# Strided convolution with norm and GELU, forward and backward: outer sums added at eviction, and a first weight-gradient combination split by batches

## The chip, the cores and the metric

The kernel runs on one core of a Trainium2 chip. The metric is the device time of one execution in microseconds (us); the time before is the median of three runs. Engines are named as in the profile: PE is TensorE's matmul, PEld its weight load, DVE is VectorE, ACT is ScalarE, POOL is GpSimd, SP is SyncE, which here issues nearly all loads.

## What is computed

```python
def _fwd_reference(x, w, gn_gamma, gn_beta):      # x (2, 16000, 256), w (31, 256, 256), bf16
    L = (T - K) // s + 1                          # K = 31, s = 2: L = 7985
    h = jnp.einsum('blc,cd->bld', x[:, 0:s * L:s, :], w[0])
    for i in range(1, K):
        h = h + jnp.einsum('blc,cd->bld', x[:, i:i + s * L:s, :], w[i])
    mu = jnp.einsum('bld->bd', h)[:, None, :] / L
    var = jnp.einsum('bld->bd', (h - mu) ** 2)[:, None, :] / L
    h = (h - mu) / jnp.sqrt(var + 1e-5)
    h = h * gn_gamma[None, None, :] + gn_beta[None, None, :]
    return _gelu(h)

_out, _vjp = jax.vjp(_f, x, w, gn_gamma, gn_beta)
_grads = _vjp(grad_out)                           # outputs: out, dx, dw, dgamma, dbeta
```

A convolution of 31 taps with stride 2 over 256 channels, a normalisation over time for each channel, and a GELU; then the gradients of x (`out_1`), w (`out_2`), gamma and beta.

## The kernel before, in words

Three large products make up the matmul work: the convolution, the input gradient and the weight gradient. Each is cut by fast-convolution splits into three branches, two halves and their sum, which the code calls A, C_ and B_ (the sum). The splits nest, so a product has branches `br` and inside each leaves `lf`. They save matmuls and cost additions: of inputs (bf16, on DVE) and of partial results (fp32, in PSUM).

The stages run in this order: F0 (convolution of batch 0), F1 (convolution of batch 1, while batch 0 is normalised and goes through GELU and its derivative), G0 (input gradient of batch 0, chunks 0 to 2, while batch 1 is normalised), G1 (chunk 3 of batch 0 and all of batch 1), and W (weight gradient, nine combinations n = 0 to 8 of two levels of branches).

**What sets the order.** One planner, `Plan`, gets every operation in program order with a guessed cost, gives each a due time, and shifts it by a table `lead` (a number for each stage, kind of operation and function that adds it) and a second table `fine` (the same by part, a chunk or a combination). Each engine's list is then sorted by the shifted times, and each engine runs its list in order. All loads and most stores go through SP's queue, which is such a list too; a load also waits until its buffer is free. PSUM is a ring of four slots of two banks (`ring`, `slots4`).

**Input gradient** (`input_grad`, from `g_leaf` to `g_evac`). For each batch b, chunk c, half chunk pr and branch br, two slots px and pt are taken. First the leaf B_ goes into px: `g_three_b` runs four matmuls into one bank, ACT copies them to the other bank (L1353), and `g_three_ac` adds eight matmuls on top. Then `g_seed` prepares px and pt as starting values of the leaves C_ and A, which add their matmuls onto them, and `g_evac` takes each of these out. For br = B_ the result is kept in GRB, an fp32 buffer in SBUF. It is the outer sum that the branches A and C_ need, and there each seed adds it: L1393 in `plus`, one addition of 128x2048 that writes px + GRB to pt and px both. `keep` is ACT's copy (L833); the evictions of A and C_ write bf16 into HO, from which the output is stored. In batch 1, and in chunk 3 of batch 0, another form is used (`outer`, `both`, sets GO and GOC), in which matmuls make part of the outer sum; the change leaves that form as it is. Where the page says that PE L1326 waits for ACT L1353, the matmul of `g_three_ac` waits for the copy.

**Weight gradient** (`weight_grad`). For each n, four tiles xt of x (two batches, two halves) and, for each batch, tiles D2 and DO of the output's gradient (`d_tile`, loaded from the DRAM buffers `dl_d`) are needed. `w_add` (L1527) forms XSUM of the two halves, 128x4096 for each batch, `pair_x` (L1625 for both batches in one, L1629 for one batch) adds neighbouring rows, `leaf_d` (L1712) and `pair_d` (L1638) form differences of the gradient, and `w_pairs` runs 2 x 16 matmuls from the pairs; `w_single` and `w_leaf` add the rest. ACT spreads the result of `w_pairs` over a slot (L1654), `w_both` (L1662) adds a middle result, and `w_emit` (L1588) adds the last two terms, writes bf16 to one of the buffers WO and stores it. `place` turns through sets of buffers for the pairs (PD). All buffers lie at hand-given addresses in one tile `arena`, so a load for n = 0 can start when the last reader of what lay at that address before is done:

```python
    XSUM_ = [[sb(o, 8, 512) for o in v] for v in ((24576, 32768), (0, 8192))]
    D2E_ = [[sb(o + 5120 * i, 10, D) for i in range(2)] for o in (0, 127424)]
    D2O_ = [[sb(o + 10240 + 4608 * i, 9, D) for i in range(2)] for o in (0, 127424)]
```

(the first set is for n = 0, the second for n = 1 to 8).

## Time and profile before

| | us |
|---|---|
| runs | 1178.08, 1179.34, 1175.58 (median 1178.08) |
| profiled execution, device time | 1176.72 |
| span of that execution | 1174.9 |
| around the span (difference) | 1.8 |
| PE busy | 1133.9 |
| DVE busy | 980.1 |
| ACT busy | 568.8 |
| mean granted clock | 0.99 |

The profiled execution lies among the three runs. Its span is what the views divide up; the 1.8 us around it are outside every view. A window's row gives for a stretch of the span the busy time of each engine with its number of instructions, then the clock that TensorE was granted (1.00 is full speed), the mean busy share of the DMA engines, and GB/s. A group's row gives line, engine, operation, written and read tiles, shapes and count, then total busy time, mean ns of one, and the idle time of that engine just before such instructions with what ended it. In a timeline the idle time ahead of a piece stands in brackets.

### The profile page before, as it was taken

Reading aid. Unit: us, or ns where it says so; the run is one execution under the profiler, and the core shown is the slowest. Engines: PE = TensorE matmul, PEld = TensorE weight load, DVE = VectorE, ACT = ScalarE, POOL = GpSimd, SP = SyncE. Lnnn points to the kernel's source line nnn. Section 1 sums busy time; section 2 is a strip of 40 time slices with the busy share of each in tenths; the row PEclk is TensorE's granted clock in tenths of the full one; section 3 lists DMA queues with packets and bytes.
Section 4 is the critical chain, followed back from the end, with each engine's and each line's share of the span. In section 5 each row is a group of like instructions: output and inputs, shape, how many; then the busy total and the mean of one; then the engine's idle time right before and its main releaser. Section 6 shows DMA issues by size and latency. Waiting matters only on the chain.

```text
span 1174.9 us, 18909 instructions
## 1 busy us (share of the span) xinstructions
PE 1133.9 (97%) x7700; PEld 755.0 (64%) x7700; DVE 980.1 (83%) x861; ACT 568.8 (48%) x849; POOL 128.3 (11%) x221
## 2 busy tenths in 40 slices
PE   5999999999999999999999999999799999899997
PEld 4888899777777954444444444444388666566784
DVE  8998787699999998898886776876699897688996
ACT  1253454778776587897854666534222212211200
POOL 0000000000000002332242223223000000000000
PEclk8999999999999999999999999999999999999999
DMA  9475747979795799999988679576987836998574
GB/s 215 69 200 101 186 135 143 213 161 212 166 230 139 266 304 264 251 255 268 233 209 219 157 181 231 133 205 162 307 234 195 289 113 203 311 328 304 167 204 126
DMA packets 345806, 243.56 MB, mean 207 GB/s; under 512 B 233377, under 2 KB 316967, under 8 KB 341543
## 3 DMA queue, kind: packets, MB, share of 16 engines
q1 hardware_dynamic: 338615, 223.47, 71.5%
q0 software_dynamic: 7104, 18.89, 5.7%
q8 instruction: 60, 0.98, 0.3%
q14 instruction: 27, 0.22, 0.1%
HBM read 106.24 MB, written 80.25 MB: 159 GB/s over the span
## 4 chain that ended last, share of the span: by engine, by line
PE 84%; DVE 7%; ACT 4%; DMA 3%; issue 2%; SPq 0%; DVEq 0%; ACTq 0%
PE ps L738 32%; PE ps L1326 27%; PE ps L1559 25%; DMA arena<-in_x_dram 2%; DVE ps L1393 2%; ACT arena L833 1%; DVE arena L696 1%; DVE arena L1393 1%; DVE arena L680 1%; ACT ps L1353 0%; ACT arena L1098 0%; DVE arena L1625 0%; DVE arena L1103 0%; DMA out_dram<-arena 0%; ACT arena L1124 0%
## 5 line engine op out<-in xcount | busy, mean ns | idle before, releaser
L1326 PE MATMUL ps<-arena 128*128 128x512 bf16 (+1 forms) x1920 | 415.6, 377 | 12.2 <-ACT ps L1353 5.0
L738 PE MATMUL ps<-arena 128*128 128x256 bf16 (+4 forms) x3460 | 406.9, 281 | 12.5 <-DVE arena L680 5.6
L738 PEld LDWEIGHTS <-arena 128*128 128x128 bf16 x3460 | 338.5, 99 | 80.8 <-DVE arena L680 6.5
L1326 PEld LDWEIGHTS <-arena 128*128 128x128 bf16 x1920 | 188.3, 98 | 238.3 <-issue 22.0
L1559 PE MATMUL ps<-arena 128*128 128x256 bf16 (+1 forms) x2320 | 312.2, 298 | 10.2 <-DVE arena L1625 8.3
L1559 PEld LDWEIGHTS <-arena 128*128 128x128 bf16 x2320 | 228.2, 99 | 94.4 <-DVE arena L1625 9.6
L833 ACT ACTIVATE arena<-ps 128x1024 f32<-128x1024 f32 (+1 forms) x143 | 145.5, 1021 | 294.6 <-PE ps L1326 108.4
L696 DVE TENSOR_TENSOR arena<-arena 128x2064 bf16<-128x2064 bf16 (+7 forms) x126 | 155.9, 1264 | 27.9 <-PE ps L738 27.4
L544 POOL DMA_DIRECT2D dld<-arena x144 | 104.7, 729 | 266.9 <-DMA arena<-arena 248.6
L1393 DVE TENSOR_TENSOR ps<-ps,arena 128x2048 f32<-128x2048 f32 x40 | 91.8, 2295 | 26.8 <-PE ps L1326 20.2
L1113 DVE TENSOR_TENSOR arena<-arena 128x2048 bf16<-128x2048 bf16 (+1 forms) x80 | 95.6, 1195 | 13.0 <-ACT arena L1107 6.4
L1527 DVE TENSOR_TENSOR arena<-arena 128x4096 bf16<-128x4096 bf16 x38 | 86.0, 2284 | 23.4 <-DMA arena<-in_x_dram 20.3
L1279 DVE TENSOR_TENSOR arena<-arena 128x1032 bf16<-128x1032 bf16 (+1 forms) x120 | 84.2, 725 | 21.9 <-PE ps L1326 16.1
L853 ACT ACTIVATE arena<-ps 128x512 bf16<-128x512 f32 (+1 forms) x64 | 37.0, 580 | 45.1 <-PE ps L738 44.4
L1654 ACT COPY ps<-ps 128x256 f32<-128x256 f32 x54 | 19.3, 357 | 79.0 <-PE ps L1559 77.3
L553 POOL MEMSET arena<- 128x128 bf16 (+11 forms) x40 | 8.4, 243 | 424.8 <-DVE arena L696 140.1
L1393 DVE TENSOR_TENSOR arena<-ps,arena 128x2048 f32<-128x2048 f32 x16 | 36.6, 2287 | 19.5 <-ACT arena L833 15.9
L808 ACT ACTIVATE arena<-ps 128x512 f32<-128x512 f32 x56 | 29.7, 601 | 38.2 <-DVE ps L818 16.3
L1638 DVE TENSOR_TENSOR arena<-arena 128x2048 bf16<-128x2048 bf16 x38 | 45.0, 1217 | 0.9 <-PE ps L1559 0.7
L1712 DVE TENSOR_TENSOR arena<-arena 128x4608 bf16<-128x4608 bf16 x18 | 45.5, 2549 | 0.0
L1103 DVE SCALAR_TENSOR_TENSOR arena<-arena 128x2048 bf16<-128x2048 bf16 (+1 forms) x16 | 35.8, 2236 | 10.9 <-ACT arena L1100 10.9
L774 ACT ACTIVATE ps<-ps 128x256 f32<-128x256 f32 x75 | 27.9, 372 | 29.4 <-PE ps L738 28.3
(80 smaller groups left out, 706.9 us busy)
## 6 DMA issues: line engine op xcount, KB each, us to landing
arena<-in_x_dram SPq DMA_DIRECT2D x40, 1024.0 KB
dld<-arena POOLq DMA_DIRECT2D x144, 128.0 KB, 3.9
arena<-hd SPq DMA_DIRECT2D x32, 512.0 KB
out_dram<-arena SPq DMA_DIRECT2D x14, 1024.0 KB
arena<-dld SPq DMA_DIRECT2D x18, 640.0 KB
arena<-dld SPq DMA_DIRECT2D x18, 576.0 KB
vl<-arena SPq DMA_DIRECT2D x36, 256.0 KB
arena<-vl SPq DMA_DIRECT2D x9, 1024.0 KB
```

The source lines that it names most:

```text
L544: lambda: e.dma_start(out=out, in_=in_), dma=np_ * ns / 16e3 * 1.03, ns=ns, tp=SH[pk], slack=slack)
L696: lambda: nc.vector.tensor_tensor(out=o, in0=a, in1=b, op=ALU.add))
L738: yield nc.tensor.matmul(ps[:, dh, cs], lhsT=wt, rhs=mv, start=s0, stop=False, skip_group_check=True)
L833: lambda: nc.scalar.activation(out=out, in_=ps, func=ACT.Copy, scale=scale))
L1113: add("DVE", dve(nf), [o], [a, b_], lambda: V.tensor_tensor(out=o, in0=a, in1=b_, op=op))
L1279: lambda: nc.vector.tensor_tensor(out=o, in0=a, in1=b, op=ALU.subtract))
L1326: yield nc.tensor.matmul(ps[:, e, 0:wide], lhsT=lt, rhs=mv, start=s0, stop=False, skip_group_check=True)
L1393: lambda: nc.vector.tensor_tensor(out=o, in0=a, in1=b, op=ALU.add))
L1527: add("DVE", dve(4096), [o], [a, b], lambda: nc.vector.tensor_tensor(out=o, in0=a, in1=b, op=ALU.add))
L1559: yield nc.tensor.matmul(ps[:, s, c0:c1], lhsT=lt, rhs=mv, start=s0, stop=False, skip_group_check=True)
L1638: add("DVE", dve(2048), [o], [u, v], lambda o=o, u=u, v=v: nc.vector.tensor_tensor(out=o, in0=u, in1=v, op=ALU.subtract))
L1712: add("DVE", dve(4608), [o], [u, v], lambda: nc.vector.tensor_tensor(out=o, in0=u, in1=v, op=ALU.subtract))
```

## The change

Three things change beside the two tables.

First, the input gradient's first batch (where neither `outer` nor `both` holds). The seed of the branches A and C_ becomes what it was for B_, a copy on ACT from px to pt, and the outer sum GRB is added at the eviction, on DVE, as PSUM is read.

```diff
-        elif br == B_:
+        else:
             keep(flat2(pt), flat2(px))
-        else:
-            o, i = both_ways()
-            plus(o, i, GRB.rearrange("p k e f -> p k (e f)"), [pt[:], px[:]], [px[:], GRB])
...
         k = (0 if br == A else 1) + (0 if lf == A else 2)
-        keep(ho[:, :, k, :], ps[:])
+        if (b, c, br) in GO or (b, c, pr) in GOC:
+            keep(ho[:, :, k, :], ps[:])
+        else:
+            g = GRB[:, 0 if lf == A else 1]
+            add("DVE", dve(1024, 1), [ho[:, :, k, :]], [ps[:], g],
+                lambda: nc.vector.tensor_tensor(out=ho[:, :, k, :], in0=ps[:], in1=g, op=ALU.add))
```

Second, the first combination of the weight gradient (n = 0) is split by batches, and its buffers lie elsewhere; for n = 1 to 8 the two halves of XSUM are no longer neighbours, so that `pair_x` runs as two instructions of 2048 there.

```diff
-    XS_ = [sb(o, 8, 512) for o in (165376, 86016, 190336, 40960)]
-    XT_ = [sb(o, 8, 512) for o in (24576, 173696, 32768, 182016)]
+    XS_ = [sb(o, 8, 512) for o in (165376, 86016, 182016, 0)]
+    XT_ = [sb(o, 8, 512) for o in (24576, 173696, 32768, 190336)]
-    XSUM_ = [[sb(o, 8, 512) for o in v] for v in ((24576, 32768), (0, 8192))]
-    D2E_ = [[sb(o + 5120 * i, 10, D) for i in range(2)] for o in (0, 127424)]
-    D2O_ = [[sb(o + 10240 + 4608 * i, 9, D) for i in range(2)] for o in (0, 127424)]
+    XSUM_ = [[sb(o, 8, 512) for o in v] for v in ((8192, 32768), (8192, 40960))]
+    D2E_ = [[sb(o, 10, D) for o in v] for v in ((24576, 40960), (127424, 132544))]
+    D2O_ = [[sb(o, 9, D) for o in v] for v in ((16384, 57344), (137664, 142272))]
...
-          for k, o, u in (("all", 16384, 73728), ("early", 110720, 118912), ("late", 57344, 65536))}
+          for k, o, u in (("all", 16384, 73728), ("early", 110720, 118912), ("late", 57344, 65536), ("first", 73728, 65536))}
...
+            if n == 0:
+                return PD[("first", "early", "late")[turn_[0] - 1]]
...
                 w_add(XSUM[b], xt[b, 0], xt[b, 1])
-            pair_x(pm, XSUM)
+                if n == 0:
+                    pair_x((pm[b],), (XSUM[b],))
+            if n:
+                pair_x(pm, XSUM)
...
+                if n == 0:
+                    for b in range(NB):
+                        o, u, v = DL[i3, b], D2[b][:, o_:o_ + 9], DO[b]
+                        add("DVE", dve(2304), [o], [u, v], lambda o=o, u=u, v=v: nc.vector.tensor_tensor(
+                            out=o, in0=u, in1=v, op=ALU.subtract))
+                    return
...
-            for h in range(2):
-                w_pairs(X[h], h, pm, DO, 1, 2)
+            if n == 0:
+                for b in range(NB):
+                    for h in range(2):
+                        w_pairs(X[h], h, pm, DO, 1, 2, True, ((b,),))
+            else:
+                for h in range(2):
+                    w_pairs(X[h], h, pm, DO, 1, 2)
...
-                        t = sb(8192 * r3 * seeded + 4096 * h, 1024, dt=FP32)
+                        t = sb((8192, 40960)[r3 * seeded] + 4096 * h, 1024, dt=FP32)
```

`w_pairs` takes the batches as groups and runs the matmuls of one group for both halves of the slot; ACT's copies follow the last group. `pair_d` runs four instructions of 1024 where the two batches' tiles lie apart (n = 0), in place of two of 2048.

Third, nearly all numbers of `lead` and `fine` are others, so the order of all stages moves. Two of their lines:

```diff
-            "G0 keep g_evac": -8.5,
-            "G0 keep g_seed": 6.5,
+            "G0 keep g_evac": -59.0,
+            "G0 keep g_seed": -46.5,
```

Below are lists of instructions as each engine runs them. Names are the tiles written and read: `ps` is PSUM, `arena` SBUF, `stats` and `esum` small tiles of the normalisation, `dld` the stored gradient in DRAM. Line numbers behind the diff's first part are higher by 4 or more in the changed kernel (L1353 becomes L1357, L1393 becomes L1397, L833 becomes L837).

ACT in G0, early in the input gradient's first batch, beside the normalisation and GELU of batch 1, before:

```order
L1098 ACTIVATE arena<-arena,stats 128x1024 x2
L1124 ACTIVATE arena,esum_116<-arena 128x1024
L833 ACTIVATE arena<-ps 128x1024
L1124 ACTIVATE arena,esum_116<-arena 128x1024
L1100 ACTIVATE arena<-arena,stats 128x1024 x2
L833 ACTIVATE arena<-ps 128x1024
L1353 COPY ps<-ps 128x512
L833 ACTIVATE arena<-ps 128x2x512
L1353 COPY ps<-ps 128x512
```

and after:

```order
L837 ACTIVATE ps<-ps 128x1024
L1128 ACTIVATE arena,esum_116<-arena 128x1024
L1104 ACTIVATE arena<-arena,stats 128x1024 x2
L837 ACTIVATE arena<-ps 128x1024 x2
L1109 ACTIVATE arena<-arena 128x2048
L1357 COPY ps<-ps 128x512
L1111 ACTIVATE arena<-arena 128x2048
L837 ACTIVATE ps<-ps 128x1024
L1102 ACTIVATE arena<-arena,stats 128x1024 x2
L1357 COPY ps<-ps 128x512
```

The evictions to bf16 (`arena<-ps 128x2x512`) are gone from ACT, and seeds (`ps<-ps 128x1024`) stand there instead; the copies of L1357 keep their place among GELU's activations.

The evictions now stand on DVE, which runs this there in the changed kernel:

```order
L1212 TENSOR_SCALAR arena<-arena,stats 128x2048
L1117 TENSOR_TENSOR arena<-arena 128x2048
L1429 TENSOR_TENSOR arena<-ps,arena 128x2x512
L1117 TENSOR_TENSOR arena<-arena 128x2048
L1283 TENSOR_TENSOR arena<-arena 128x2x2x258
L1117 TENSOR_TENSOR arena<-arena 128x2048
L1429 TENSOR_TENSOR arena<-ps,arena 128x2x512
```

L1429 is the new eviction, one for each leaf, among the products of GELU's derivative (L1117) and the gradient's plane sums (L1283).

DVE at the junction of the input gradient and the weight gradient (the last branches of batch 1, then n = 0), before:

```order
L1393 TENSOR_TENSOR ps<-ps,arena 128x2x1024 x2
L1393 TENSOR_TENSOR arena<-ps,arena 128x2048
L1393 TENSOR_TENSOR ps<-ps,arena 128x2048
L1393 TENSOR_TENSOR arena<-ps,arena 128x2048
L1629 TENSOR_TENSOR arena<-arena 128x2048
L1393 TENSOR_TENSOR ps<-ps,arena 128x2048
L1527 TENSOR_TENSOR arena<-arena 128x4096
L1629 TENSOR_TENSOR arena<-arena 128x2048
L1527 TENSOR_TENSOR arena<-arena 128x4096
L1625 TENSOR_TENSOR arena<-arena 128x4096
L1712 TENSOR_TENSOR arena<-arena 128x4608 x2
```

and after:

```order
L1397 TENSOR_TENSOR ps<-ps,arena 128x2x1024 x2
L1533 TENSOR_TENSOR arena<-arena 128x4096
L1635 TENSOR_TENSOR arena<-arena 128x2048
L1397 TENSOR_TENSOR arena<-ps,arena 128x2048
L1397 TENSOR_TENSOR ps<-ps,arena 128x2048
L1397 TENSOR_TENSOR arena<-ps,arena 128x2048
L1397 TENSOR_TENSOR ps<-ps,arena 128x2048
L1635 TENSOR_TENSOR arena<-arena 128x2048
L1533 TENSOR_TENSOR arena<-arena 128x4096
L1635 TENSOR_TENSOR arena<-arena 128x2048
L1646 TENSOR_TENSOR arena<-arena 128x1024 x4
L1731 TENSOR_TENSOR arena<-arena 128x2304 x4
```

The first XSUM (L1533, before L1527) and a pair sum of one batch (L1635, before L1629) stand ahead of the last four seeds, nothing stands between these, and the pair sum of both batches (L1625) is now one of each batch.

SP's queue at the same place, before:

```order
L544 DMA arena<-in_x_dram 128x8x512
L549 DMA_TRANSPOSE arena<-arena 128x4x128 x2
L544 DMA arena<-dld_0_80 128x2304
L544 DMA arena<-dld_0_89 128x2304
L544 DMA arena<-in_x_dram 128x8x512 x2
L544 DMA arena<-dld_0_80 128x2560
L544 DMA arena<-dld_0_89 128x2560
```

and after:

```order
L548 DMA arena<-dld_0_80 128x2304
L548 DMA arena<-in_x_dram 128x8x512 x2
L553 DMA_TRANSPOSE arena<-arena 128x4x128 x2
L548 DMA arena<-dld_0_89 128x2304
L548 DMA arena<-dld_0_80 128x2560
L548 DMA arena<-dld_0_89 128x2560
```

The two loads of x now stand ahead of the last two transposes and of one load of the gradient.

402 lines of the change are left out of this document (207 added, 195 removed).

## The prediction

> **What bounds the kernel now.** I read the page first (how full each engine is), then the windows (where TensorE is not full), then TensorE's waits and timeline (who ends each gap), and last the DVE, SP and chain views around the widest gap.
>
> ```profile
> span 1174.9 us, 18909 instructions
> PE 1133.9 (97%) x7700; PEld 755.0 (64%) x7700; DVE 980.1 (83%) x861; ACT 568.8 (48%) x849; POOL 128.3 (11%) x221
> 300.00:400.00 100.00, 100.00 (x796) 77.36 (x794) 94.70 (x103) 67.96 (x111) 3.67 (x11) 1.00 0.70 177
> 410.00:470.00 60.00, 58.32 (x323) 31.46 (x322) 52.08 (x63) 47.61 (x70) 9.01 (x15) 1.00 0.98 285
> 470.00:530.00 60.00, 57.87 (x270) 26.21 (x268) 54.55 (x56) 53.12 (x65) 21.87 (x36) 1.00 0.95 254
> 530.00:590.00 60.00, 57.98 (x272) 26.31 (x270) 49.93 (x50) 48.32 (x53) 15.73 (x23) 1.00 1.00 249
> 590.00:650.00 60.00, 58.28 (x273) 26.63 (x272) 46.35 (x65) 28.33 (x37) 19.39 (x31) 1.00 0.79 207
> 830.00:860.00 30.00, 22.84 (x123) 13.05 (x122) 25.82 (x15) 6.99 (x12) 1.44 (x2) 0.89 1.05 323
> 1000.00:1100.00 100.00, 95.08 (x619) 61.04 (x618) 82.78 (x49) 15.47 (x23) 0.00 (x0) 0.98 0.85 283
> 1150.00:1175.00 25.00, 18.82 (x127) 12.22 (x125) 13.69 (x12) 0.00 (x0) 0.00 (x0) 0.95 0.38 107
> ```
>
> The first two are the page's; the others are windows (length, then busy time and count of PE, PEld, DVE, ACT, POOL, then granted clock, DMA share, GB/s). PE is the bound: it is idle for 1174.9 − 1133.9 = 41.0 us in all. The change does not alter a matmul, so it can gain only from idle time and from time at a lower clock. The idle time is where the change works: 240 − 232.45 = 7.55 us in 410 to 650 (the input gradient's first batch), 7.16 in 830 to 860 (the junction with the weight gradient, clock 0.89), 4.92 in 1000 to 1100, 6.18 at the end. In the forward pass (300 to 400) PE has no idle time at all, with DVE at 94.7%.
>
> TensorE's waits (total, times, longest) and its timeline (start, length, work, and the idle time ahead):
>
> ```profile
> PE ps L1559 <- DVE arena L1625: 8.3, 2, 4.9
> PE ps L1326 <- ACT ps L1353: 5.0, 7, 0.9
> PE ps L1326 <- DVE ps L1393: 5.0, 7, 2.3
> PE ps L1326 <- ACT arena L833: 1.2, 5, 0.2
> ...
> 463.82 26.55 PE L1326 MATMUL ps<-arena 128*128 128x256 bf16 x124 [0.74 <-DVE ps L1393]
> 520.95 19.01 PE L1326 MATMUL ps<-arena 128*128 128x512 bf16 x88 [0.74 <-ACT ps L1353]
> 841.11 5.30 PE L1326 MATMUL ps<-arena 128*128 128x512 bf16 x16 [2.30 <-DVE ps L1393]
> 851.27 8.94 PE L1559 MATMUL ps<-arena 128*128 128x256 bf16 x65 [4.87 <-DVE arena L1625]
> 1028.85 41.69 PE L1559 MATMUL ps<-arena 128*128 128x256 bf16 x240 [3.48 <-DVE arena L1625]
> 1071.16 97.65 PE L1559 MATMUL ps<-arena 128*128 128x256 bf16 x768 [0.62 <-ACT arena L833]
> ```
>
> The first batch loses its time in many short waits for ScalarE's copy and DVE's seed; the weight gradient loses it in two long waits for a pair sum (L1625), which itself waits for x. The long gaps cost twice, as windows of PE alone show (busy, clock, DMA share, GB/s):
>
> ```profile
> 841.00:846.00 5.00, 4.89 (x15) 0.66 0.99 339
> 851.00:856.00 5.00, 4.73 (x28) 0.66 0.95 339
> 1070.00:1075.00 5.00, 4.38 (x41) 1.00 0.89 243
> ```
>
> Behind the gaps of 2.30 and 4.87 us the clock is 0.66 over 5 us: (1 − 0.66) × 5 = 1.7 us lost each time. Behind the gap of 0.62 it stays 1.00.
>
> The Trainium skill, "TensorE: Matmul & The Clock Gate", section "Why this matters for your kernels", puts the fall to half clock at gaps of more than about 3 us. The row at 841 us shows it behind 2.30, so I go by the row; by the page the junction would give back one loss of 1.7 us, not two, and the sum below would be 10.3 in place of 12.0.
>
> **Part 1, the first batch.** Rows by form (busy us, mean ns, idle time):
>
> ```profile
> L1393 DVE TENSOR_TENSOR ps<-ps,arena 128x2048 f32<-128x2048 f32 x40 | 91.8, 2295 | 26.8 <-PE ps L1326 20.2 <-ACT arena L1389 5.6 <-ACT arena L833 0.4
> L833 ACT ACTIVATE arena<-ps 128x1024 bf16<-128x1024 f32 x64 | 65.2, 1021 | 84.4 <-PE ps L1326 84.4
> L1588 DVE TENSOR_TENSOR arena<-ps,arena 128x1024 bf16<-128x1024 f32 x15 | 18.2, 1220 | 10.7 <-DMA out_dram<-arena 5.6 <-PE ps L1559 5.0
> L833 ACT ACTIVATE ps<-ps 128x1024 f32<-128x1024 f32 x13 | 13.1, 1008 | 12.8 <-PE ps L1326 5.8 <-PE ps L1559 5.5 <-PE ps L738 1.4
> L1103 DVE SCALAR_TENSOR_TENSOR arena<-arena 128x2048 bf16<-128x2048 bf16 (+1 forms) x16 | 35.8, 2236 | 10.9 <-ACT arena L1100 10.9
> ```
>
> (L1103 mixes two forms, so its 2236 is a mean.) Sixteen double seeds on DVE go (16 × 2.295 = 36.7 us) and 16 keeps on ScalarE come (16 × 1.008 = 16.1). 32 evictions leave ScalarE (32 × 1.021 = 32.7) and come to DVE as an addition that reads PSUM and writes bf16; before has that very form at L1588, so 32 × 1.220 = 39.0. DVE gets 2.3 us more, ScalarE 16.5 less. Neither is the bound: DVE's 202.9 busy us of 240 become 205.2. What counts is what PE waits for. A seed becomes 1.3 us shorter. In the orders of the two kernels, the copy L1353 has no matmul between the four that it copies from and the one that waits for it at 6 places of the input gradient before, and at 1 after; seeds with only eight matmuls of cover go from 2 to 0, and second-batch evictions with too little cover from 5 to 3. So 5/6 of the copies' 5.0 us goes (4.2), two seed waits like that of 0.74 (1.5), and 2/5 of 1.2 (0.5). Against it stands one new sum of gradient planes on DVE (`third`) without cover at the start of the stage, put at 0.8, about what one of those copies cost. Gain 4.2 + 1.5 + 0.5 − 0.8 = **5.4**. Bounds: 7.55, all the idle time of the four windows, and nothing, if DVE's evictions, which now stand among GELU operations of up to 2.24 us, give as much back. At nothing I cost the 2.3 us of DVE: its 37 idle us in these windows hide them; without that cover they cost 2.3. GRB is now read up to the last eviction of its half chunk, so the sum that writes it next may start one unit later; that sum is short and is first needed by an eviction, not by a matmul, so I cost that at nothing too (one 1.22 each time, if it were ahead of a seed).
>
> **Part 2, the junction.** DVE, SP's queue, and the chain of waits:
>
> ```profile
> 833.02 2.30 DVE L1393 TENSOR_TENSOR ps<-ps,arena 128x2048 f32<-128x2048 f32 x1 [1.83 <-PE ps L1326]
> 835.42 2.29 DVE L1393 TENSOR_TENSOR arena<-ps,arena 128x2048 f32<-128x2048 f32 x1
> 837.63 1.22 DVE L1629 TENSOR_TENSOR arena<-arena 128x2048 bf16<-128x2048 bf16 x1
> 838.76 2.29 DVE L1393 TENSOR_TENSOR ps<-ps,arena 128x2048 f32<-128x2048 f32 x1
> 846.60 2.29 DVE L1527 TENSOR_TENSOR arena<-arena 128x4096 bf16<-128x4096 bf16 x1 [2.21 <-DMA arena<-in_x_dram]
> 848.92 2.29 DVE L1625 TENSOR_TENSOR arena<-arena 128x4096 bf16<-128x4096 bf16 x1
> ...
> 825.75 4.09 SPq L549 DMA_TRANSPOSE arena<-arena  x2
> 834.35 3.31 SPq L544 DMA_DIRECT2D arena<-in_x_dram  x2
> ...
> 837.12 9.46 DMA arena<-in_x_dram
> ```
>
> Two things are late before. A pair sum of one batch (L1629) stands ahead of the last seed, and two x loads go out at 834.35, behind two transposes (4.09 us) and behind memory that comes free late; the first load takes 9.46, then a sum (2.29) and the double pair sum (2.29) follow before PE goes on at 851.27. After the change XSUM and D2E, D2O lie elsewhere, the x loads stand ahead of those transposes, and by the order 13.6 us of matmuls (counted at 0.216 each, or half for 256 columns) lie between the load's place and the first matmul that needs it (4.3 before). That matmul needs batch 0 alone: load 9.46 + sum 2.29 + single pair sum 1.22 = 12.97, within 13.6. So the 4.87 go, with their 1.7 of clock. The 2.30 lose L1629's 1.22, leaving 1.1; but a sum and such a pair sum (2.29 + 1.22) move ahead of the four seeds where DVE idles 1.83, so up to 1.7 comes on top. I take 1.5 left over, nearer the low end since another idle stretch of DVE lies just ahead. Whether 1.5 brings the half clock lies between 0.62 (no) and 2.30 (yes): half of 1.7. Gain: 7.16 + 2 × 1.7 − 1.5 − 0.85 = **8.2**. Bounds 10.6 (all) and 0.
>
> The splits cost DVE instructions: the fixed part of one is 2 × 1.217 − 2.284 = 0.15 us, by the forms of 2048 and 4096 elements. Four to six more in the first combination (0.6 to 0.9) and one more in each of the eight others (1.2) lie beside PE's work there; with that cover gone, 2.1.
>
> **Part 3, the rest of the weight gradient.**
>
> ```profile
> 1020.84 4.62 DVE L1527 TENSOR_TENSOR arena<-arena 128x4096 bf16<-128x4096 bf16 x2 [4.30 <-DMA arena<-in_x_dram]
> 1170.06 1.56 DVE L1588 TENSOR_TENSOR arena<-ps,arena 128x1024 bf16<-128x1024 f32 x2 [3.40 <-DMA out_dram<-arena]
> ```
>
> At the sixth combination x is late again (4.30, and 3.48 on PE). By the order, two loads in series fit 14.0 us of matmuls before and 14.5 after: gain **0.5**, bounds 5.2 (3.48 and 1.7 of clock) and −3.0. At the end DVE waits 3.40 for the store that frees its output buffer; after the change that store is issued before two transposes, not behind them. PE's last matmul ends at 1071.16 + 97.65 = 1168.81, 1.25 before the last additions start, so the gain lies between 1.25, if both additions wait for it, and 3.40: I take **1.9**, bounds 0 and 3.4. The forward pass is only reordered: 0, bounds ±3, from DVE's 94.7% there.
>
> **Allowance.** Before has three waits over 2 us that the order alone does not show, so I take off one such wait with its clock, 2.3 + 1.7 = **4.0**.
>
> **Sum.** 5.4 + 8.2 + 0.5 + 1.9 − 4.0 = 12.0. The profiled execution took 1176.72 (span 1174.9 and 1.8 around it): 1164.7. The median of the runs, 1178.08, is 1.36 above it: **1166.0**.
>
> **Rivals.** *DVE becomes late in the first batch (slower).* Evictions queue behind GELU work on an engine that is 91% busy in 470 to 530 (54.55 of 60), PSUM's slot comes free late, and PE waits for it. A slot comes back after the three others of PSUM's ring, at least 3 × 8 matmuls of 19.01 / 88 = 0.216 us, 5.2 us, less 1.22 for the eviction: it decides once the queue ahead of an eviction exceeds about 4 us, one L1103 (2.24) and two shorter ones. If half of the 16 units then lose one L1103 each, 8 × 2.24 = 17.9; with 8.2 + 0.5 + 1.9 gained, 7.3 slower: 1185.4. Against it: ScalarE's release and a 1.3 us shorter seed in the same units. *The x wait moves on:* the loads go earlier, but the next pair of loads, at the fourth combination, has 20.7 us by the order for two in series, 18.9 at 9.46 each; a DMA share of 1.05 in 830 to 860 speaks for lateness. Then part 2 is lost again: 5.4 + 0.5 + 1.9 − 4.0 = 3.8, about 1174. *The change does not do what it says:* the short waits only change their releaser (GELU evictions for copies), and the new wait takes the junction's place: no more than 1 us gained, 1177.
>
> **Chances.** Forecast 0.58 (own range 1158 to 1173), moved x wait 0.15, no change 0.09, DVE late 0.18. Under 0.3% (3.5 us) a measurement of this kernel cannot tell from no change. Faster: 0.58 and two thirds of 0.15, 0.68. Same: the other third and 0.09, 0.14. Slower 0.18. The range leaves out most of the slower case and a little at the low end: 1157 to 1180.
>
> **What would show it.** Right: in the input gradient's first batch L1353 and L1393 all but vanish from PE's waits and the idle time falls from 7.55 to about 2; in the junction DVE's wait for x is gone, one gap under 2 us stays, and no half clock or one; DVE's last additions start within 1 us of PE's end. Wrong: PE waits for DVE's evictions in the first batch; a wait for x over 2 us anywhere in the weight gradient besides the sixth combination; idle time in the forward pass. Above 1174.5 the forecast has failed, and the gap that took the time must be in one of these places.

## The result, and the profile after

The changed kernel takes 1165.84 us (median of 4 runs, 1160.24 to 1167.0) against 1178.71 for the kernel before in the same comparison (4 runs, 1175.58 to 1183.06). The ratio is 0.9879, with a 95% interval from 0.9833 to 0.9925: 1.2% faster, and the forecast was 1166.0. The profiled execution took 1166.96, its span is 1165.2, so 1174.9 − 1165.2 = 9.7 us of span went. The medians lie 12.9 apart, the profiled executions 9.8 (1176.72 and 1166.96), within the scatter of the runs. Only part of the time went where the forecast had it go.

The page of the changed kernel, its first two lines, then the windows that were shown of before (length, busy time and count of PE, PEld, DVE, ACT, POOL, granted clock, DMA share, GB/s):

```profile
span 1165.2 us, 18856 instructions
PE 1128.7 (97%) x7645; PEld 753.8 (65%) x7700; DVE 982.8 (84%) x892; ACT 553.3 (47%) x833; POOL 134.8 (12%) x221
```

```profile
410.00:470.00 60.00, 56.38 (x327) 32.35 (x332) 50.53 (x65) 49.12 (x80) 13.63 (x13) 1.00 0.94 292
470.00:530.00 60.00, 58.27 (x269) 26.77 (x274) 55.88 (x61) 49.34 (x59) 20.13 (x32) 1.00 0.98 254
530.00:590.00 60.00, 56.76 (x256) 25.72 (x260) 48.70 (x53) 40.31 (x45) 19.39 (x30) 0.97 1.03 252
590.00:650.00 60.00, 58.03 (x269) 26.59 (x273) 44.70 (x63) 29.61 (x38) 17.68 (x28) 1.00 0.81 208
830.00:860.00 30.00, 28.28 (x176) 17.17 (x176) 28.21 (x20) 9.87 (x15) 1.44 (x2) 1.00 1.00 275
1000.00:1100.00 100.00, 98.37 (x646) 63.47 (x651) 89.76 (x58) 17.14 (x27) 0.00 (x0) 1.00 0.83 278
```

In 830 to 860 PE's idle time fell from 7.16 to 1.72 and the clock from there is 1.00; in 1000 to 1100 it fell from 4.92 to 1.63. In 410 to 650 it rose, from 7.55 to 10.56 (the first window reaches into the forward pass here, which ends later), and the clock shows 0.97 in one of the four.

Windows at fixed times mix stages that shift. A sharper account counts weight loads: each matmul has one, all 7700 are in every trace, and the order says which stage each belongs to. The time from one group of matmuls' first weight load to the next group's is put down to the stage of the first. "dx" is the input gradient, "junction" the last chunk of batch 1 and the weight gradient's combination n = 0, and F1 starts, as in the planner, behind the first branch of its chunk 0. Times are in us:

```
stage                       before     after   after - before
F0                           211.0     212.3       +1.3
F1 chunk 0                    38.4      40.2       +1.8
F1 chunks 1-3                169.7     173.1       +3.4
dx batch 0                   227.3     226.7       -0.6
dx batch 1, chunks 0-2       144.6     144.3       -0.3
junction                      93.4      84.6       -8.8
W n=1-3                      105.0     105.7       +0.7
W n=4-5                       79.2      74.0       -5.2
W n=6-7                       67.1      67.1        0.0
W n=8, end                    39.4      37.2       -2.2
```

So the weight gradient and its junction gained 15.5 us, the first batch of the input gradient, where the first edit sits, gained 0.6, and the forward pass, whose code is the same, lost 6.5.

**First batch.** The first edit acts on all four chunks of batch 0. Chunk 3 has the plain form too, in both kernels (16 double seeds before, four in each chunk); the form with `outer` and `both` is used in batch 1 alone.

TensorE's waits between 413 and 660 of the kernel before (total, times, longest), and between 417 and 660 of the changed one:

```profile
PE ps L1326 <- ACT ps L1353: 5.0, 7, 0.9
PE ps L1326 <- DVE ps L1393: 1.7, 3, 0.7
PE ps L1326 <- ACT ps L833: 0.6, 2, 0.3
```

```profile
PE ps L1330 <- DVE arena L1429: 2.8, 1, 2.8
PE ps L1330 <- ACT ps L837: 2.6, 4, 1.0
PE ps L1330 <- DVE arena L1283: 1.8, 2, 1.0
PE ps L1330 <- ACT ps L1357: 0.4, 1, 0.4
```

The waits for copies (L1353, now L1357) are gone but for 0.4, and those for DVE's seeds are gone, as planned. Waits for ACT's new seeds (L837), for plane sums (L1283) and one for the new eviction (L1429) stand in their place: 7.3 us before, 7.6 after. The long one, in DVE's timeline and TensorE's:

```profile
556.62 1.22 DVE L1117 TENSOR_TENSOR arena<-arena 128x2048 bf16<-128x2048 bf16 x1 [2.06 <-ACT arena L1109]
561.75 1.23 DVE L1429 TENSOR_TENSOR arena<-ps,arena 128x1024 bf16<-128x1024 f32 x1 [3.91 <-DMA out_dram<-arena]
```

```profile
563.03 3.45 PE L1330 MATMUL ps<-arena 128*128 128x512 bf16 x9 [2.83 <-DVE arena L1429]
```

DVE stood still for 3.91 us, because its list runs in order and the eviction had to wait for the store that empties HO, which SP had issued only at 553.73, behind a transposing load that took SP 5.15 us; PE then waited 2.83 for the PSUM slot. The clock of 0.97 over the window from 530 is (1 − 0.97) × 60 = 1.8 us more.

**Junction.** TensorE's timeline of the changed kernel, then DVE's and SP's:

```profile
840.27 5.13 PE L1330 MATMUL ps<-arena 128*128 128x512 bf16 x24 [0.71 <-ACT ps L1357]
845.88 1.02 PE L1330 MATMUL ps<-arena 128*128 128x512 bf16 x4 [0.49 <-DVE ps L1397]
846.75 1.91 PE L1565 MATMUL ps<-arena 128*128 128x256 bf16 x16
```

```profile
845.74 1.22 DVE L1635 TENSOR_TENSOR arena<-arena 128x2048 bf16<-128x2048 bf16 x1
847.05 2.29 DVE L1533 TENSOR_TENSOR arena<-arena 128x4096 bf16<-128x4096 bf16 x1
849.38 1.22 DVE L1635 TENSOR_TENSOR arena<-arena 128x2048 bf16<-128x2048 bf16 x1
```

```profile
833.98 1.84 SPq L548 DMA_DIRECT2D arena<-in_x_dram  x2
835.92 6.71 SPq L553 DMA_TRANSPOSE arena<-arena  x2
```

Two gaps of 0.71 and 0.49 are left of 2.30 and 4.87. DVE goes from one operation to the next without a bracket: it waits for no x. The x loads are out at 833.98, 12.8 us ahead of the first pair matmuls at 846.75 (834.35 and 16.9 ahead before, when those matmuls came at 851.27 after a wait), and the transposes stand behind them.

**Sixth combination (n = 5) and end.** DVE and TensorE of the changed kernel:

```profile
1011.00 1.23 DVE L1635 TENSOR_TENSOR arena<-arena 128x2048 bf16<-128x2048 bf16 x1
1012.14 2.28 DVE L1533 TENSOR_TENSOR arena<-arena 128x4096 bf16<-128x4096 bf16 x1
1017.53 4.62 DVE L1533 TENSOR_TENSOR arena<-arena 128x4096 bf16<-128x4096 bf16 x2 [3.11 <-DMA arena<-in_x_dram]
1022.18 1.23 DVE L1635 TENSOR_TENSOR arena<-arena 128x2048 bf16<-128x2048 bf16 x1
...
1159.63 1.56 DVE L1594 TENSOR_TENSOR arena<-ps,arena 128x1024 bf16<-128x1024 f32 x2 [1.75 <-PE ps L1565]
1161.37 0.42 DVE L1594 TENSOR_TENSOR arena<-ps,arena 128x256 bf16<-128x256 f32 x1 [0.19 <-PE ps L1565]
```

```profile
1023.47 39.87 PE L1565 MATMUL ps<-arena 128*128 128x256 bf16 x233 [0.80 <-DVE arena L1635]
1063.68 97.65 PE L1565 MATMUL ps<-arena 128*128 128x256 bf16 x764 [0.34 <-ACT arena L837]
```

At n = 5 DVE still waits for x (3.11 here, 4.30 before), but PE waits 0.80 in place of 3.48. Before, from the landing to PE it took two sums, another operation and a double pair sum, 4.62 + 1.22 + 2.28 = 8.1 us; now one pair sum is done at 1011.00, ahead of the wait, and 4.62 + 1.23 = 5.9 are left. At the end DVE's last additions wait for PE alone, and the last starts at 1161.37, when PE ends (1063.68 + 97.65 = 1161.33).

### The profile page after: what moved, and what is told of

It reads as the page before. It is cut to its first block, busy times and chain, and to the rows that moved or that the text cites. A ratio compares the mean times of both kernels' runs of the same rounds, so it can differ in the third digit from the quotient of the medians.

```text
span 1165.2 us, 18856 instructions
## 1 busy us (share of the span) xinstructions
PE 1128.7 (97%) x7645; PEld 753.8 (65%) x7700; DVE 982.8 (84%) x892; ACT 553.3 (47%) x833; POOL 134.8 (12%) x221
## 5 line engine op out<-in xcount | busy, mean ns | idle before, releaser
L1330 PEld LDWEIGHTS <-arena 128*128 128x128 bf16 x1920 | 188.2, 98 | 236.0 <-issue 16.9
L1565 PE MATMUL ps<-arena 128*128 128x256 bf16 (+1 forms) x2305 | 308.6, 296 | 3.6 <-DVE arena L1635 1.9
L1565 PEld LDWEIGHTS <-arena 128*128 128x128 bf16 x2320 | 226.7, 98 | 85.6 <-DVE arena L1635 3.0
L837 ACT ACTIVATE arena<-ps 128x1024 f32<-128x1024 f32 (+1 forms) x111 | 113.0, 1022 | 242.6 <-PE ps L1565 84.1
L700 DVE TENSOR_TENSOR arena<-arena 128x2080 bf16<-128x2080 bf16 (+7 forms) x126 | 156.5, 1265 | 26.1 <-PE ps L742 25.5
L1117 DVE TENSOR_TENSOR arena<-arena 128x2048 bf16<-128x2048 bf16 (+1 forms) x80 | 95.6, 1195 | 11.5 <-ACT arena L1109 6.0
L1533 DVE TENSOR_TENSOR arena<-arena 128x4096 bf16<-128x4096 bf16 x38 | 86.5, 2284 | 6.2 <-DMA arena<-in_x_dram 5.7
L1283 DVE TENSOR_TENSOR arena<-arena 128x1032 bf16<-128x1032 bf16 (+1 forms) x120 | 84.1, 725 | 8.3 <-PE ps L1330 5.2
L1397 DVE TENSOR_TENSOR ps<-ps,arena 128x2048 f32<-128x2048 f32 x24 | 55.1, 2297 | 25.2 <-PE ps L1330 24.4
L1429 DVE TENSOR_TENSOR arena<-ps,arena 128x1024 bf16<-128x1024 f32 x32 | 38.8, 1218 | 12.9 <-PE ps L1330 7.6
L1397 DVE TENSOR_TENSOR arena<-ps,arena 128x2048 f32<-128x2048 f32 x16 | 36.6, 2289 | 14.5 <-ACT arena L837 10.9
L1736 DVE TENSOR_TENSOR arena<-arena 128x4608 bf16<-128x4608 bf16 x16 | 40.4, 2551 | 8.5 <-PE ps L1565 7.8
L1232 ACT COPY arena<-arena 128x768 bf16<-128x768 bf16 (+1 forms) x64 | 36.2, 615 | 18.6 <-DVE arena L1223 14.8
```

The costliest lines, as they stand in the source:

```text
L700: lambda: nc.vector.tensor_tensor(out=o, in0=a, in1=b, op=ALU.add))
L837: lambda: nc.scalar.activation(out=out, in_=ps, func=ACT.Copy, scale=scale))
L1117: add("DVE", dve(nf), [o], [a, b_], lambda: V.tensor_tensor(out=o, in0=a, in1=b_, op=op))
L1283: lambda: nc.vector.tensor_tensor(out=o, in0=a, in1=b, op=ALU.subtract))
L1330: yield nc.tensor.matmul(ps[:, e, 0:wide], lhsT=lt, rhs=mv, start=s0, stop=False, skip_group_check=True)
L1397: lambda: nc.vector.tensor_tensor(out=o, in0=a, in1=b, op=ALU.add))
```

## The experiments

### Switching one part of the change off, or on alone, and letting the planner sort

Four kernels took one part of the change out or put one in; the planner then made its order anew from the tables. In all experiments the kernel before was run again beside the new one; its medians lie between 1177.88 and 1178.78, so times of different experiments can be compared.

The changed kernel, with the numbers of F0 and F1 from before in both tables:

```diff
-            "F1 f_mm f_leaf": -458.5,
+            "F1 f_mm f_leaf": -272.5,
...
-            "F1 ve f_seed": 8.0,
+            "F1 ve f_seed": -48.0,
```

> The changed kernel with the old numbers of both tables for the convolution stages (F0, F1) and all else as changed. In the changed kernel's profile those two stages take 6.3 us more than before, though no operation of theirs was edited. Theory: the new order of these stages costs it; then they fall back by about 6 us, the later stages stay within 1 us, and the span is about 1159 (time about 1160). Rival: it is the scatter of one execution (the four runs of the changed kernel lie between 1160.24 and 1167.0); then the stages stay where they are or move by less than 2 us, time 1164 to 1167.

Measured: 1184.71, ratio to before 1.0049 (1.0027 to 1.0071). F1's chunks 1 to 3 took 180.1, against 169.7 before and 173.1 after; neither the theory nor the rival. The input gradient's stages, whose numbers are the changed ones, grew as well (233.7 and 150.4, in place of 226.7 and 144.3). The old numbers in a program with other operations behind them do not give the old order.

The changed kernel with the old seed and eviction:

```diff
-        else:
-            keep(flat2(pt), flat2(px))
+        elif br == B_:
+            keep(flat2(pt), flat2(px))
+        else:
+            o, i = both_ways()
+            plus(o, i, GRB.rearrange("p k e f -> p k (e f)"), [pt[:], px[:]], [px[:], GRB])
...
-        if (b, c, br) in GO or (b, c, pr) in GOC:
-            keep(ho[:, :, k, :], ps[:])
-        else:
...
+        keep(ho[:, :, k, :], ps[:])
```

> The changed kernel with the old seed and eviction in the first batch of the input gradient; tables and weight gradient as changed. Theory A (the prediction's): adding at eviction is worth about 5 us there, so the first batch gets about 5 us longer, time about 1171. Theory B (from the changed kernel's windows, where the first batch is no shorter than before): the edit itself brings nothing, because waits for the seed's keep and for the eviction's addition replace those for the copy; the first batch stays within 2 us, time 1164 to 1168.

Measured: 1230.2, ratio 1.0427 (1.0385 to 1.0468): neither theory. The first batch took 289.7 in place of 226.7. TensorE's longest waits:

```profile
PE ps L1330 <- ACT arena L837: 24.5, 11, 9.9
PE ps L1330 <- DVE ps L1397: 13.5, 10, 3.7
```

PE now waits for evictions on ScalarE, once for 9.9 us. They are sorted by a number that the change had set when only the B_ evictions of the first batch were of that kind (`G0 keep g_evac`, −8.5 before, −59.0 now); that this number does it was not tried alone.

The kernel before with the new seed and eviction alone (the diff above, turned round):

> The kernel before with the new seed and eviction alone, old tables, old weight gradient. Theory A: first batch about 5 us shorter, time about 1173. Theory B: no gain, first batch within 2 us, time 1176 to 1181. A third way: the old numbers place the new evictions badly on DVE, and the first batch gets longer by more than 4 us (time above 1182); then the new tables are needed for the edit.

Measured: 1206.59, ratio 1.0228 (1.0183 to 1.0272): the third way. The first batch took 236.0 (227.3 before), but F1 also went from 208.1 to 220.7 and the chunks of batch 1 from 144.6 to 152.9, though no operation there had changed.

The changed kernel with the old code of the weight gradient (from XS_ to the end of `weight_grad`):

> The changed kernel with the old code of the weight gradient (old places, no split by batches), new tables and new seed. Theory: the junction's gain (10.0 us from the last chunk of the input gradient to the end of the first combination) comes from the places that are free earlier and the split, so it is lost, and so is the sixth combination's 5.2 us if it comes from XSUM's new place; time about 1181 if both, 1176 if the junction alone. Rival: the new tables make it (they set when loads are issued); then the time stays within 3 us of 1166.

Measured: 1216.28, ratio 1.0306 (1.0259 to 1.0354): above the theory and the rival. The junction took 104.8, worse than before's 93.4, and batch 1's chunks 162.9 in place of 144.3.

Each of the four is slower than both kernels. What this shows is not the worth of a part: the planner's simulated clock runs through the whole program, so an edit can re-sort stages far from it (with the new seed and eviction alone, the convolution's operations, which are the same, came out in another order on four of the five engines), and tables and code fit each other only as a pair. To price a part, the order had to be held.

### The order held

In the other kernels `order` returns a written list of the operations. Where an operation would stand ahead of one that it depends on, that one goes ahead too.

```diff
     def order(self):
-        ops = self.ops
...
-        return sorted(range(n), key=lambda i: (self.start[i], i))
+        return list(map(int, SEQ.split()))
```

Convolution and input gradient with before's code and list, weight gradient with the changed code and list, merged by the number of matmuls issued (nothing had to be moved):

> Orders held by an explicit list, so that no edit re-sorts the rest: convolution and input gradient with the code and order of before, weight gradient with the code and order of the change. Theory: all of the gain comes from the weight gradient and its junction (in the two profiles 10.0 us from the last chunk to the end of the first combination, 5.2 at the sixth, 2.2 at the end), and the rest of the change loses 7.7; then the span is 1174.9 - 17.4 = 1157.5, time about 1159, faster than both kernels. Rival: the junction needs the new order of the input gradient too; then the 10.0 us do not come and the time is about 1169.

Measured: 1162.64 (1162.42 to 1162.84), ratio 0.9864 (0.9837 to 0.9892): the theory, less its size. The span is 1160.7, not 1157.5; the theory counted 17.4 for the weight gradient, where the account by weight loads has 15.5, and 1.2 more of the difference came at F0. Its stages:

```
stage                       before     after   new W alone   old W, rest new
F0                           211.0     212.3       212.2          212.1
F1 chunk 0                    38.4      40.2        38.4           40.1
F1 chunks 1-3                169.7     173.1       169.7          172.7
dx batch 0                   227.3     226.7       227.3          224.6
dx batch 1, chunks 0-2       144.6     144.3       145.1          143.9
junction                      93.4      84.6        84.6          105.5
W n=1-3                      105.0     105.7       105.7          106.1
W n=4-5                       79.2      74.0        73.0           78.2
W n=6-7                       67.1      67.1        67.1           67.1
W n=8, end                    39.4      37.2        37.7           39.5
```

The whole gain is there without the first edit and without the new order of the convolution, and F1 is as fast as before. F0's 1.2 us more came with F0's old list, so in the changed kernel nothing speaks for the new order as the cause of its 1.3.

The reverse, old weight gradient under the changed stages (last column):

> The reverse, orders held: convolution and input gradient as changed, weight gradient with the code and order of before. Theory: the gain is lost and the 7.7 us of loss stay, time about 1184 (1166.9 + 17.4). Rival: the old weight gradient works as well under the new stages, since its loads only need the queue free earlier; time below 1175.

Measured: 1199.04 (1191.6 to 1201.5; the profile is that of the 1191.6), ratio 1.0162 (1.0121 to 1.0203). The gain is lost, and more than the theory's 1184 says: the junction takes 105.5. TensorE waits there 12.86 us for the double pair sum, whose x DVE gets late (4.51), and 4.60 for the pair differences, which DVE can write only when a store is done (9.73 us of standing still). Why the memory came free later under this order was not followed further.

The kernel before with 16 seeds and 32 evictions exchanged in place:

> The kernel before in its own order, with the 16 seeds and 32 evictions exchanged in place (three instructions moved because the eviction now reads the outer sum). Theory A (prediction): the seeds' waits of 0.7 go and evictions wait for nothing; the first batch 1 to 2 us shorter, time about 1177. Theory B: DVE's evictions stand in a queue that was ordered for ScalarE's, and hold PSUM's slots; first batch 5 us or more longer, time above 1183. Either way it tells how much of the 28 us of the run with the edit alone came from re-sorting.

Measured: 1187.13, ratio 1.0062 (1.0039 to 1.0085). First batch 233.0, 5.7 more than before: theory B by the time, but only in part by its cause. Of the 31.5 us of span that the edit alone cost with a re-sorted order (1206.4 − 1174.9), the edit in place makes at most 10.2 (1185.1 − 1174.9, of which 1.7 is F0's start); the rest was re-sorting. One line of TensorE's waits:

```profile
PE ps L1396 <- ACT ps L1423: 10.0, 10, 2.9
```

The copies' waits (L1423 is L1353 there) are twice as long as before, where ScalarE's list now has the new seeds in it too; for DVE's evictions, which theory B names, TensorE waits 2.8.

The changed kernel with the convolution in before's order:

> The changed kernel with the operations of the convolution (F0, F1) in the order of before and all others in the changed order, lists held. Theory: the 6.3 us that these stages lost come from their new order; span about 1159, time about 1161. Rival: the last 3.5 of them (end of F1, where the input gradient's first sums and copies start) come from what the new first batch asks of DVE there, and stay: time about 1164.

Measured: 1165.56 (1160.74 to 1166.99), ratio 0.9882 (0.985 to 0.9913). F1's chunk 0 is back at 38.4: its 1.8 us were the order's. Chunks 1 to 3 stay at 172.8: the 3 us at the end of F1 come from what stands around it, the start of the input gradient, as the rival said (TensorE waits there 1.21, 0.43 and 0.86 us for DVE). The total is nearly the same, since F0 took 1.1 more and the first batch 1.0 more. The first batch's long wait is another one here: 5.52 us for a seed of ScalarE, which had itself stood still 7.19 us for POOL. So the place that loses most in this stage changes with the order around it.

### Which part of the new weight gradient

Both from the list with the new weight gradient alone. First, batch 0's matmuls of n = 0 not ahead of batch 1's sums:

```diff
 SEQ, operations of n = 0 by name
-  w_mm w_pairs (batch 0, h = 1)
...
-  w_mm w_pairs (batch 0, h = 0)
...
+  w_mm w_pairs (batch 0, h = 0)
+  w_mm w_pairs (batch 0, h = 1)
   w_mm w_pairs (batch 1, h = 0)
```

> The run with the new weight gradient alone, but batch 0's two groups of pair matmuls of the first combination moved behind batch 1's pair sum, as if not split; places and everything else stay. Theory: the split matters, since batch 1's sum and pair sum (2.29 + 1.22) now stand on the path with nothing for PE to do: 2 to 5 us more at the junction, time 1165 to 1168. Rival: the earlier places alone do it; within 1 us of 1162.6.

Measured: 1161.94 (1160.54 to 1162.26), ratio 0.986 (0.9834 to 0.9885), junction 84.6. The split of the matmuls by batches is worth nothing here: the rival, as far as the split goes. (The sums on DVE stay split.)

Second, all buffers at the places of before:

```diff
-    XSUM_ = [[sb(o, 8, 512) for o in v] for v in ((8192, 32768), (8192, 40960))]
-    D2E_ = [[sb(o, 10, D) for o in v] for v in ((24576, 40960), (127424, 132544))]
-    D2O_ = [[sb(o, 9, D) for o in v] for v in ((16384, 57344), (137664, 142272))]
+    XSUM_ = [[sb(o, 8, 512) for o in v] for v in ((24576, 32768), (0, 8192))]
+    D2E_ = [[sb(o + 5120 * i, 10, D) for i in range(2)] for o in (0, 127424)]
+    D2O_ = [[sb(o + 10240 + 4608 * i, 9, D) for i in range(2)] for o in (0, 127424)]
...
```

> The run with the new weight gradient alone, its split and list kept, but all buffers at the places of before (XS_, XT_, XSUM_, D2E_, D2O_, PD, the middle tile). Theory: the loads of x are issued as early in the list but wait for memory, so the junction gets back 8 to 13 us, time 1171 to 1176; and if the sixth combination's wait (3.5 and half clock) returns too, 5 more, 1176 to 1181. Rival: the list alone made the gain; within 2 us of 1162.6.

Measured: 1179.86, ratio 1.0018 (1.0004 to 1.0032). TensorE and DVE at the junction:

```profile
846.10 3.57 PE L1396 MATMUL ps<-arena 128*128 128x512 bf16 x8 [5.85 <-DVE ps L1463]
861.58 18.66 PE L1629 MATMUL ps<-arena 128*128 128x256 bf16 x144 [6.36 <-DVE arena L1715]
```

```profile
849.51 2.29 DVE L1597 TENSOR_TENSOR arena<-arena 128x4096 bf16<-128x4096 bf16 x1 [2.34 <-DMA arena<-in_x_dram]
860.29 2.36 DVE L1715 TENSOR_TENSOR arena<-arena 128x2048 bf16<-128x2048 bf16 x2 [7.23 <-DMA out_dram<-arena]
```

The junction takes 100.7, 16.1 more: DVE waits for x (2.34) and 7.23 us to write its pair differences (L1715) where a store of the input gradient still reads, and seeds queue behind work that came too early. Behind each of PE's two gaps the clock is 0.50 for 6.83 us, together 6.8 us of the 16.1. So the places are what makes the junction's new order possible; the new places under the old order were not tried, so what they give by themselves stays open. n = 4 and 5 take 74.4, against 73.0 with the new places and 79.2 before: most of that gain is the list's. DVE and TensorE there:

```profile
1028.41 4.62 DVE L1597 TENSOR_TENSOR arena<-arena 128x4096 bf16<-128x4096 bf16 x2 [4.02 <-DMA arena<-in_x_dram]
1033.06 2.29 DVE L1695 TENSOR_TENSOR arena<-arena 128x4096 bf16<-128x4096 bf16 x1
```

```profile
1035.41 38.28 PE L1629 MATMUL ps<-arena 128*128 128x256 bf16 x224 [1.20 <-DVE arena L1695]
```

With the old places the pair sum is one instruction again, 2.29 in place of 1.23 behind the landing of x, and DVE waits 4.02 for x; PE's gap is 1.20, where the kernel with the new places, from which this one was made, has none (1.78 is DVE's wait there) and the changed kernel 0.80. What the list took out of that path is the operation of 1.22 that stood ahead of the pair sum before; the rest of the way from 3.48 to 1.20, about 1.1, is by subtraction that x lands earlier against PE's work.

### The waits for the copy by themselves

The first term of the prediction said that uncovered copies cost what TensorE waits for them. Two kernels from the list with the new weight gradient alone, old seeds and evictions, put work over the copy. First, leaves from behind `g_three_ac` to ahead of it:

```diff
 SEQ, operations by name, at six places of the first batch
   g_mm g_three_b
+  g_mm g_leaf        (8 matmuls)
   g_mm g_three_ac
   g_mm g_three_ac
-  g_mm g_leaf        (8 matmuls)
```

> The run with the new weight gradient alone (1162.64), and in its list six groups of eight matmuls of a leaf moved, each from just behind a waiting g_three_ac to just ahead of it, so that they stand between the four matmuls that the copy reads and the ones that wait for it; seed and eviction stay as in the kernel before, nothing else moves. It tests the prediction's first term by itself: six uncovered copies at 0.7 to 0.95 us each. Theory: they go, 4.4 us, time about 1158.2. Rival: the time comes back at the next seed or eviction, since DVE and ScalarE stay as late; time above 1161.5.

Measured: 1177.84, ratio 0.9995 (0.9981 to 1.0009): 15 us slower than without the move, the rival and more. TensorE's waits and its timeline at the first of the six places:

```profile
PE ps L1396 <- DVE ps L1463: 16.9, 10, 3.3
PE ps L1396 <- ACT ps L1423: 1.4, 3, 0.6
```

```profile
437.29 14.37 PE L1396 MATMUL ps<-arena 128*128 128x256 bf16 x60 [2.79 <-DVE ps L1463]
```

The copies' waits fell from 5.0 to 1.4, the seeds' rose from 4.5 to 16.9 (L1463 is L1393), and behind four of the longer gaps the clock fell to half, 1.7 us each. What the copy's wait had covered is seen in the kernel that this one was made from, at the same place, on ScalarE, DVE and TensorE:

```profile
432.67 1.01 ACT L903 ACTIVATE arena<-ps 128x1024 f32<-128x1024 f32 x1
433.58 0.59 ACT L1423 COPY ps<-ps 128x512 f32<-128x512 f32 x1
```

```profile
433.71 4.73 DVE L1463 TENSOR_TENSOR ps<-ps,arena 128x2048 f32<-128x2048 f32 x2 [0.39 <-ACT arena L903]
```

```profile
434.22 30.07 PE L1396 MATMUL ps<-arena 128*128 128x512 bf16 x140 [0.95 <-ACT ps L1423]
```

ScalarE first takes the outer sum out (L903), then copies; the outer sum releases DVE's seed at 433.71, which ends at about 436.0 (half of 4.73). TensorE, held 0.95 us by the copy, runs eight matmuls (1.73) and reaches the leaf at 434.22 + 1.73 = 435.95. The two arrive together. Without the wait for the copy there is a wait for the seed.

Second, the copy under the leaf before it, with no leaf, seed or eviction moved against another:

```diff
 SEQ, operations by name, at four places of the first batch
+  g_mm g_three_b
+  copy of g_three_b (ACT)
   g_mm g_leaf        (8 matmuls)
...
-  g_mm g_three_b
-  copy of g_three_b (ACT)
   g_mm g_three_ac
```

> The run with the new weight gradient alone (1162.64), and in its list four groups g_three_b with their copies moved ahead of the leaf before them, so that the copy runs under that leaf's matmuls; no leaf, seed or eviction moves against another. Counting waits says: the copy's waits of 0.95, 0.74, 0.74 and 0.74 go, 3.2 us, time 1159.5. The other reading, from the rows around them (last leaf of B_ ends, ScalarE keeps its result 1.02, DVE's seed 2.29, next leaf: 3.3 us, while TensorE has 4 + 8 matmuls and the copy's wait, 0.87 + 0.74 + 1.73 = 3.3): the seed ends as the copy's detour does, so each wait comes back on the seed as 3.3 - 1.73 = 1.6 us, of which 0.87 was spent earlier; nothing gained, time within 1 us of 1162.6.

Measured: 1169.04 (1166.93 to 1171.91), ratio 0.9924 (0.9902 to 0.9945). Nothing was gained, and 6.4 us were lost where the second reading said at most 1. At two of the four places the wait came back on the seed as 1.72, where 1.6 was expected, at the other two as 2.74 and 2.56:

```profile
437.73 28.22 PE L1396 MATMUL ps<-arena 128*128 128x256 bf16 x129 [2.74 <-DVE ps L1463]
497.52 3.06 PE L1396 MATMUL ps<-arena 128*128 128x256 bf16 x10 [2.56 <-DVE ps L1463]
529.77 17.00 PE L1396 MATMUL ps<-arena 128*128 128x256 bf16 x78 [1.72 <-DVE ps L1463]
560.17 28.26 PE L1396 MATMUL ps<-arena 128*128 128x256 bf16 x130 [1.72 <-DVE ps L1463]
```

So the second reading holds at the two places where ScalarE's keep and DVE's seed had little ahead of them, and is too kind at the other two: at the first, ScalarE loaded a table (1.28) ahead of the keep, at the second it ran a GELU activation (1.91), and DVE a product (1.23) ahead of the seed. The 6.2 us of the first batch (233.5 against 227.3) are those waits and some half clock.

## Why the prediction was right, and where it was not

The time was right, within 0.2 us, but by terms that failed in both directions. Part of the match is luck of the runs as well: the forecast was made from the profiled execution, 12.0 us less, and the two profiled executions differ by 9.8.

- **First batch, 5.4 forecast, 0.6 measured.** TensorE's idle time in the four windows was to fall from 7.55 to about 2 and rose to 10.56. The step that failed is "5/6 of the copies' 5.0 us goes (4.2), two seed waits like that of 0.74 (1.5)": it took a wait's length for its worth. The copies' and seeds' waits did go, but the two moves of the copies alone, under the old seeds, showed that the next matmul's other input, the seed, comes no earlier than the copy's detour ends. In the changed kernel waits for other inputs (ACT's seeds 2.6, plane sums 1.8, an eviction 2.8) add up to as much as before.
- **DVE late in the first batch.** The place was right, at one spot (2.83 us and 1.8 of clock). So one of the forecast's own signs of being wrong came. The cause was another: DVE's queue was not too full, DVE stood still and waited for HO's store. In before's own order the edit cost 5.7 us there.
- **Junction, 8.2 forecast, 8.8 measured.** The mechanism held: earlier places, x loads ahead of the transposes, no wait for x, no half clock. Of the terms, 1.5 left over was 0.71 + 0.49, and the 0.85 of clock did not come. The reason given for the cover, that the first matmul needs batch 0 alone, is not what did it: without that split the junction is the same. (The sum of 10.3 that the prediction sets beside its own still takes off the 0.85, though by the rule it follows there a gap of 1.5 brings no half clock; it would be 11.2. Nothing else rests on it.)
- **n = 5, 0.5 forecast, 5.2 measured** (for n = 4 and 5), at its upper bound. The term was mis-sized: I counted the matmuls between loads, where the path from the landing of x to PE on DVE had become 2.2 us shorter (5.9 in place of 8.1), half by an operation moved out of it and half by the split of L1625, which I had put down as a cost of 0.15. The gap went from 3.48 to 0.80, and the half clock behind it went too.
- **End, 1.9 forecast, 2.2 measured.** Right.
- **Forward pass, 0 forecast (bounds ±3), 6.5 lost.** The step that failed is "the forward pass is only reordered: 0". 1.3 came at the start, where the old order showed as much in other kernels; 1.8 is the new order of F1's first chunk, with a wait of 1.61 for ScalarE, and 3.4 is the end of F1, which stays with the old order of its own operations, with a wait of 1.90 for DVE. The kernel before has no gap over 1.2 us in F1.
- **Allowance, 4.0 off.** It was not derived from a place, and it is what made the sum right: 4.8 too much in the first batch and 6.5 in the forward pass, against 4.7 too little at n = 5, 0.6 at the junction, 0.3 at the end and the 4.0. A right total is no proof of its terms.

The version with the new weight gradient alone beats before by 1.4%. Its runs and those without the split lie at 1160.54 to 1162.84, eight of them, and the changed kernel's at 1160.24 to 1167.0; the intervals of the ratios overlap, so that it beats the changed kernel too is likely and not settled.

## What to carry to other kernels

A wait is worth at most the time until the waiting engine's next input is ready. Before a wait is counted as gain, follow the other inputs of the next few operations; where an engine's queue serves both, removing one wait may lengthen the other past the point where the clock falls. When a planner sorts the whole program, hold the order before pricing one part; and look at where buffers lie: the same list of operations took 17 us more with the buffers at their old places (1179.86 against 1162.64).

## What was not expected of the hardware

Gaps on TensorE of like length differ in what follows. In the last kernel the gap of 2.74 us left the clock at full speed, that of 2.56 did not. The clock in the traces shows why. In all fourteen, half clock comes in stretches of 3.41 us or whole multiples of it (but for the one that the end of the kernel cuts off), and within a trace all these stretches lie on one grid. The gap of 2.56 lies inside one stretch of its grid, from 494.67 to 498.08; that of 2.74 is split over two. The rows show these stretches and the ones behind them (length, PE busy, clock, DMA share, GB/s):

```profile
494.67:498.08 3.41, 0.85 (x6) 1.00 0.57 185
498.08:501.49 3.41, 3.19 (x10) 0.50 0.72 85
433.23:436.64 3.41, 1.76 (x9) 1.00 1.18 161
436.64:440.05 3.41, 2.32 (x13) 1.00 0.73 118
```

PE is idle for 3.41 − 0.85 = 2.56 us of the first, and half clock follows; it is idle for 1.65 of the third and 1.09 of the fourth, and full clock follows. Counted in this way over the fourteen traces, from 60 us on, a stretch at full clock with up to 1.94 us idle was followed by full clock every time, one with 2.06 us or more by half clock all 46 times, and the four in between were mixed. A stretch of half clock costs 3.41 / 2 = 1.7 us, as the prediction had it from the rows at 841 and 851. The Trainium skill, "TensorE: Matmul & The Clock Gate", section "What's actually happening", says that the activity window is about 3.4 us long and runs freely, so that the point at which the clock changes depends on where in it the first matmul lands; these rows agree, and show the like for a gap.

Identical orders of the convolution's start also differ: F0 took 211.0 in the kernel before and 212.2 to 213.4 in the seven kernels that run it in the same order.
